# Column-tiled denominators, a layer norm scale moved into the residual, and a re-ordered head and tail in a linear-attention kernel

## The chip, the cores and the metric

The kernel runs on one core of a Trainium2 chip. The metric is device time in microseconds (us); lower is better. The engines are called TensorE (PE in the profile, its weight loads PEld), VectorE (DVE), ScalarE (ACT), GpSimd (POOL) and SyncE (SP, which issues 51 of the 53 DMA transfers that the profile of the kernel before lists).

One execution of a program on one core is called fast or slow by its time alone: slow is over 1.5% above the fastest run of the same kernel. Each run records its span on the core and the mean clock granted to TensorE, as a share of full speed. The product "span times (1 − granted clock)" is called the *clock loss* below: the time that TensorE would have had more at full clock. It is a derived number, not a measured delay, and E12 shows that part of it costs no time.

## The reference, cut to what matters

Two layers, each a linear attention (A) and a one-token feed-forward (B), on 2048 tokens of width 512, with 32 heads of 16.

```python
def _A_ref(x, wqkv, wo):
    q, k, v = ...                                    # x @ wqkv, split into 32 heads of 16
    phi = lambda t: jnp.where(t > 0, t + 1, jnp.exp(t)) + 1e-6
    pq, pk = phi(q), phi(k)
    kv = jnp.einsum("bhsd,bhse->bhde", pk, v)
    z = jnp.einsum("bhsd->bhd", pk)
    num = jnp.einsum("bhqd,bhde->bhqe", pq, kv)
    den = jnp.einsum("bhqd,bhd->bhq", pq, z)[..., None] + 1e-6
    return heads_back(num / den) @ wo
def _B_ref(x, w_r, w_gate, w_up, w_down):
    r = x @ w_r                                      # one token is chosen: the largest r
    ...                                              # gather it, y = (silu(xs@w_gate) * (xs@w_up)) @ w_down
    return x + scatter(y * sigmoid(r_sel))           # y is added to that token alone
x = A_x
x = x + _A_ref(_layernorm(x), A_wqkv, A_wo)
x = x + _B_ref(_layernorm(x), B_w_r, B_w_gate, B_w_up, B_w_down)
x = x + _A_ref(_layernorm(x), A_wqkv, A_wo)          # layer 1, as layer 0
x = x + _B_ref(_layernorm(x), B_w_r, B_w_gate, B_w_up, B_w_down)
```

## The kernel before: the parts that matter

Every operation is recorded with its engine; a printed list of numbers (`ORDER`) then fixes the order on each engine, and another the PSUM banks. So "moving" an operation means another list.

The denominators of 512 queries come from four matmuls that sum into one PSUM bank. The weights `Zr` are padded to 128 columns, so each matmul uses the full width (128*128 in the profile below) although it fills only 32 rows of the result that differ from zero.

```python
def den(e):
    for m in (3, 0, 1, 2):
        ins = e.matmul(B(db), Zr[:, m, :, :].rearrange("p a b -> p (a b)"), pqT[:, m, cols],
                       start=(m == 3), stop=(m == 2))
...                                     # then log and exp(-) on ScalarE: lden, rden
for m in range(NC_D):                   # per group: four broadcasts by matmul, four multiplies on VectorE
    A("pe",  ... e.matmul(B(bb), sel[:, m, :], rden[:, j, :], start=True, stop=True) ...)
    A("dve", ... e.tensor_tensor(pqT[:, m, cols], pqT[:, m, cols], B(bb), ALU.mult) ...)
```

A feed-forward returns its own input, the layer norm, with the one token changed, and that is added to the residual stream. So after layer 0's feed-forward (the middle layer norm) `x` is scaled and shifted on GpSimd, for all 16 tiles of 128 tokens; later layer 1's attention output is added on VectorE.

```python
# middle layer norm, GpSimd, 16 tiles: x = x * (1 + 1/sd) - mean/sd
A("pool", ... e.tensor_scalar(x_tok[:, t, :], x_tok[:, t, :], us[:, t:t + 1], nmr[:, t:t + 1],
                              op0=ALU.mult, op1=ALU.add) ...)
# residual of a layer, VectorE
A("dve", ... e.scalar_tensor_tensor(out=x_tok[:, t, :], in0=B(ob), scalar=1.0, in1=x_tok[:, t, :],
                                    op0=ALU.mult, op1=ALU.add, accum_out=s1[L][:, t:t + 1]) ...)
```

The last row of the output is turned from a column into one row of 512 by four matmuls, copied from PSUM, and stored at an index that SyncE first loads into a register.

```python
for c in range(NC_D):
    ins = e.matmul(B(ob)[0:1, c * P:(c + 1) * P], xout_col[:, c:c + 1], ident[:, :], start=True, stop=True)
e.tensor_copy(row_out[:], B(ob)[0:1, :])            # 1 x 512
e.reg_load(reg_sp, idxu[0:1, 0:1]); iv = e.snap(reg_sp)
e.dma_start(out_rows[bass.ds(iv, 1), :], row_out[0:1, :])
```

## Time and profile before

| | before |
|---|---|
| time, median of 3 runs | 185.92 us (185.80 to 185.97) |
| profiled run | 184.34 us, span 182.5 us, granted clock 0.947 |
| TensorE / VectorE / GpSimd busy | 165.0 / 138.3 / 88.2 us |

The page of the profile of the kernel before: the span; the busy time of each engine; TensorE's busy tenths and its granted clock in 40 slices of 4.56 us; and one costly group (line, engine, operation, output and inputs, shapes, count, then busy us and mean ns, then idle us before it and what ended it).

```profile
span 182.5 us, 3799 instructions
...
PE 165.0 (90%) x1379; PEld 87.0 (48%) x1398; DVE 138.3 (76%) x423; ACT 109.5 (60%) x275; POOL 88.2 (48%) x144
...
PE   7999999999999977999999999999999799971691
...
PEclk9999999999999999999999999699999999997555
...
L773 POOL TENSOR_SCALAR x_tok<-x_tok,us,nmr 128x512 bf16<-128x512 bf16 x16 | 12.2, 774 | 0.9 <-DVE stat L770 0.9
...
```

TensorE is busy 90% of the span, and the holes that show in its row are, with slices counted from 0, the first, 14 and 15 (64 to 73 us), 31 (141 to 146 us) and four of the last five. The clock row shows a 6 in one slice near 116 us and 5 at the end, which is half speed. The group at the end is the GpSimd scaling that the change takes away from 14 of the 16 tiles: 774 ns each.

Windows view of the kernel before: for each stretch its length, then busy us of each engine with the instruction count, then the granted clock, the DMA share and GB/s.

```profile
...
core 0: us, PE busy (x) PEld busy (x) DVE busy (x) ACT busy (x) POOL busy (x), PEclk, DMA share, GB/s
65.00:71.00 6.00, 3.85 (x17) 1.45 (x17) 5.49 (x18) 4.54 (x18) 0.00 (x0) 1.00 0.01 3
114.00:119.00 5.00, 4.76 (x109) 3.90 (x107) 1.89 (x5) 1.21 (x4) 1.99 (x4) 0.66 0.01 3
119.00:125.00 6.00, 5.92 (x78) 3.89 (x77) 4.35 (x16) 3.16 (x8) 1.30 (x3) 1.00 0.01 3
165.00:180.00 15.00, 7.97 (x239) 7.25 (x239) 9.18 (x49) 3.36 (x15) 6.75 (x13) 0.55 0.39 142
...
```

From 65 to 71 us TensorE is busy 3.85 of 6.00 us while VectorE is busy 5.49. Of the 2.15 us that TensorE is idle, 1.23 end when ScalarE delivers the reciprocal `rden` of a denominator group whose matmuls had just run, and 0.87 end with a broadcast multiply on VectorE. From 114 to 119 us the clock is 0.66: a part of this stretch ran at half. At 165 to 180 us, the tail, the clock is 0.55 and TensorE works on one-column matmuls.

Timeline of TensorE in the kernel before, at the first denominator group of layer 0 (start, duration, engine, line, operation, count). The four denominator matmuls overlap (each is recorded at 379 ns, the four together at 1.03 us), so what a group costs is the distance to the next start.

```profile
...
start us, us, engine line op out<-in xcount [idle before <-releaser]
...
54.78 1.03 PE L676 MATMUL ps<-pqT,Zr 128*128 128x512 bf16 x4
55.64 0.59 PE L564 MATMUL ps<-wo,kvT 128*128 128x512 bf16 x2
...
```

The next matmul starts 0.86 us after the group's start (55.64 − 54.78).

Timeline of the end of the kernel before:

```profile
...
178.02 0.16 DVE L1048 TENSOR_TENSOR xout_col<-xcol,ps 128x4 bf16<-128x4 f32 x1 [1.75 <-PE ps L871]
...
178.24 0.58 PE L1055 MATMUL ps<-ident,xout_col 128*1 128x128 bf16 x4 [0.25 <-DVE xout_col L1048]
178.86 0.68 DVE L1059 CAST row_out<-ps 1x512 bf16<-1x512 f32 x1 [0.68 <-PE ps L1055]
180.24 0.32 SPq L1065 DMA_DIRECT2D out_dram<-row_out  x1
```

After the column is ready at 178.18, the four matmuls, the copy of 1x512 (0.68 us) and the register load stand before the store at 180.24.

### The profile page before, as it was taken

The page shows a single profiled execution, that of the slowest core. Times are in us where ns is not written, and L with a number is a line of the kernel's source. Part 1 is how long each engine was busy: PE and PEld are TensorE (multiplying, and loading weights), DVE is VectorE, ACT ScalarE, POOL GpSimd, SP SyncE. Part 2 cuts the span into 40 slices and gives each one's busy share as a digit, 9 for nine tenths or more (in the row PEclk, how much of TensorE's full clock was granted, in tenths as well). Part 3 has the DMA queues.
Part 4 walks back from the last instruction along what each step waited for, and adds up shares of the span by engine and source line. Part 5 has one row for each costly group of instructions (what it writes and reads, how often), then busy time and mean ns, then how long its engine had stood idle before and what let it go on. Part 6 is the DMA issues. An engine that isn't in the chain of part 4 may idle for free.

```text
span 182.5 us, 3799 instructions
## 1 busy us (share of the span) xinstructions
PE 165.0 (90%) x1379; PEld 87.0 (48%) x1398; DVE 138.3 (76%) x423; ACT 109.5 (60%) x275; POOL 88.2 (48%) x144
## 2 busy tenths in 40 slices
PE   7999999999999977999999999999999799971691
PEld 2344455444454423444455458774454244440680
DVE  7866788865789989889587657367488989899811
ACT  2297556586659568888968653236668346496110
POOL 4359468955552103338999997316152120009320
PEclk9999999999999999999999999699999999997555
DMA  5999224799920000222442200000000000003630
GB/s 153 328 384 176 25 59 86 204 269 370 380 77 0 0 4 0 57 59 57 86 90 58 59 4 0 4 4 0 2 4 0 0 0 0 0 4 115 230 122 0
DMA packets 23107, 15.83 MB, mean 87 GB/s; under 512 B 15633, under 2 KB 21522, under 8 KB 22962
## 3 DMA queue, kind: packets, MB, share of 16 engines
q1 hardware_dynamic: 23010, 15.47, 29.8%
q0 software_dynamic: 80, 0.13, 0.7%
q8 instruction: 11, 0.18, 0.4%
q14 instruction: 6, 0.05, 0.1%
HBM read 9.83 MB, written 2.10 MB: 65 GB/s over the span
## 4 chain that ended last, share of the span: by engine, by line
PE 78%; DVE 8%; POOL 5%; ACT 3%; DMA 2%; issue 2%; DVEq 0%
PE ps L514 27%; PE ps L596 15%; PE ps L702 15%; PE ps L531 4%; PE ps L676 4%; PE ps L849 3%; POOL xn_tok L636 3%; PE ps L687 3%; DVE pqT L689 2%; PE ps L812 2%; DMA x_tok<-in_A_x_dram 2%; PE ps L871 2%; POOL Eb L494 1%; DVE st L643 1%; ACT junk L711 1%
## 5 line engine op out<-in xcount | busy, mean ns | idle before, releaser
L514 PE MATMUL ps<-wqkv,xnT 128*128 128x512 bf16 x247 | 58.8, 379 | 0.6
L494 POOL TENSOR_SCALAR Eb<-Eb 128x512 bf16<-128x512 bf16 x64 | 39.9, 630 | 40.2 <-ACT Eb L492 37.3
L492 ACT ACTIVATE Eb<-ps 128x512 bf16<-128x512 f32 x64 | 37.7, 597 | 22.6 <-PE ps L596 10.4
L514 PEld LDWEIGHTS ps<-wqkv,xnT 128*128 128x128 bf16 x256 | 23.6, 97 | 24.9 <-issue 0.2
L596 PE MATMUL ps<-xnT,wqkv 128*128 128x512 bf16 x122 | 31.3, 385 | 0.6 <-DVE pk L496 0.2
L702 PE MATMUL ps<-Mw,pqT 128*128 128x512 bf16 x125 | 29.1, 379 | 1.2 <-DVE pqT L689 1.1
L496 DVE SCALAR_TENSOR_TENSOR pk<-ps,Eb 128x512 bf16<-128x512 f32 x32 | 21.6, 687 | 10.4 <-POOL Eb L494 8.4
L496 DVE SCALAR_TENSOR_TENSOR pqT<-ps,Eb 128x512 bf16<-128x512 f32 x32 | 21.6, 686 | 7.1 <-POOL Eb L494 6.9
L521 ACT ACTIVATE va<-ps 128x512 bf16<-128x512 f32 x32 | 19.2, 600 | 9.0 <-PE ps L514 6.2
L711 ACT ACTIVATE junk<-x_tok 128x512 bf16<-128x512 bf16 x32 | 19.9, 622 | 7.0 <-DVE x_tok L707 6.5
L707 DVE SCALAR_TENSOR_TENSOR x_tok<-ps,x_tok 128x512 bf16<-128x512 f32 x32 | 21.7, 689 | 3.1 <-PE ps L702 1.9
L689 DVE TENSOR_TENSOR pqT<-pqT,ps 128x512 bf16<-128x512 bf16 x32 | 20.3, 680 | 1.2 <-PE ps L687 1.2
L702 PEld LDWEIGHTS ps<-Mw,pqT 128*128 128x128 bf16 x128 | 12.1, 97 | 15.7 <-DVE pqT L689 1.7
L596 PEld LDWEIGHTS ps<-xnT,wqkv 128*128 128x128 bf16 x128 | 11.9, 99 | 13.7 <-issue 1.0
L636 POOL TENSOR_SCALAR xn_tok<-x_tok,cs,nms 128x512 bf16<-128x512 bf16 x16 | 12.2, 773 | 12.3 <-DVE nms L756 11.7
L636 POOL TENSOR_SCALAR xn_tok<-x_tok,rs,nms 128x512 bf16<-128x512 bf16 x14 | 11.6, 840 | 8.0 <-DVE nms L655 4.8
L773 POOL TENSOR_SCALAR x_tok<-x_tok,us,nmr 128x512 bf16<-128x512 bf16 x16 | 12.2, 774 | 0.9 <-DVE stat L770 0.9
L531 PE MATMUL ps<-va,pk 128*128 128x129 bf16 x128 | 11.9, 227 | 0.3 <-DVE pk L496 0.3
L531 PEld LDWEIGHTS ps<-va,pk 128*128 128x128 bf16 x128 | 9.3, 101 | 4.9 <-DVE pk L496 0.5
L687 PE MATMUL ps<-rden,sel 128*128 128x512 bf16 x32 | 9.3, 381 | 2.0 <-ACT rden L683 1.2
L643 DVE BATCH_NORM_STATS2 st<-x_tok 128x6 f32<-128x512 bf16 x16 | 10.1, 674 | 0.1
L1034 POOL TENSOR_SCALAR xn_tok<-x_tok,us,stat 128x512 bf16<-128x512 bf16 x9 | 7.0, 790 | 3.1 <-DVE us L1026 2.9
(191 smaller groups left out, 193.4 us busy)
## 6 DMA issues: line engine op xcount, KB each, us to landing
out_dram<-xn_tok SPq DMA_DIRECT2D x8, 256.0 KB, 2.1
wu<-in_B_w_up_dram SPq DMA_DIRECT2D x2, 896.0 KB, 8.7
wd<-in_B_w_down_dram SPq DMA_DIRECT2D x2, 896.0 KB, 7.1
wg<-in_B_w_gate_dram SPq DMA_DIRECT2D x2, 896.0 KB, 11.5
wqkv<-in_A_wqkv_dram SPq DMA_DIRECT2D x3, 512.0 KB, 7.8
x_tok<-in_A_x_dram SPq DMA_DIRECT2D x1, 1024.0 KB, 9.9
x_tok<-in_A_x_dram SPq DMA_DIRECT2D x2, 256.0 KB, 3.5
x_tok<-in_A_x_dram SPq DMA_DIRECT2D x1, 512.0 KB
```

Of the source, the lines that this page charges most:

```text
L492: A("act", lambda e: e.activation(Eb[:, i, :], src(), ACTF.Exp), reads=[b, "table"], writes=[f"E{i}"], est=600, name=name + "E")
L494: A("pool", lambda e: e.tensor_scalar(Eb[:, i, :], Eb[:, i, :], 1.0, 0.0, op0=ALU.min, op1=ALU.max), reads=[f"E{i}"], writes=[f"E{i}"], es ...
L496: return A("dve", lambda e: e.scalar_tensor_tensor(out=dst, in0=src(), scalar=1e-6, in1=Eb[:, i, :], op0=ALU.max, op1=ALU.add), reads=[b, ...
L514: ins = e.matmul(B(b), xT[:, c, t * P:(t + 1) * P], wqkv[:, c, lo:lo + D], start=(c == 0), stop=(c == NC_D - 1))
L521: A("act", lambda e: e.activation(va[:, i, :].rearrange("p (m k) -> p m k", k=129)[:, :, 0:P], B(vb).rearrange("p (m k) -> p m k", k=P), A ...
L531: ins = e.matmul(views[m], pk[:, i, m * P:(m + 1) * P], va[:, i, m * 129:(m + 1) * 129], start=(first and m in (0, 3)), stop=False, skip_g ...
L596: ins = e.matmul(B(qb), wqkv[:, c, qc * P:(qc + 1) * P], xnT[L][:, c, tg * 512:(tg + 1) * 512], start=(c == 0), stop=(c == NC_D - 1))
L636: A("pool", lambda e: e.tensor_scalar(xn_tok[:, t, :], x_tok[:, t, :], scale[:, t:t + 1], nbias[:, t:t + 1], op0=ALU.mult, op1=ALU.add), r ...
L689: A("dve", (lambda e, m=m, bb=bb: e.tensor_tensor(pqT[:, m, cols], pqT[:, m, cols], B(bb), ALU.mult)), reads=[bb, f"pq{tg}_{m}"], writes=[ ...
L702: ins = e.matmul(B(ob), pqT[:, m, t * P:(t + 1) * P], Mw[:, m, :], start=(m == 0), stop=(m == NC_D - 1))
L707: A("dve", lambda e: e.scalar_tensor_tensor(out=x_tok[:, t, :], in0=B(ob), scalar=1.0, in1=x_tok[:, t, :], op0=ALU.mult, op1=ALU.add, accu ...
L711: A("act", lambda e: e.activation(junk[:, j, :], x_tok[:, t, :], ACTF.Square, accum_out=s2[L][:, t:t + 1]), reads=[f"x{t}", "table"], writ ...
```

## The change

The intent: give each of a group's four denominator matmuls 32 of the 128 columns, so that four run at once; take 14 of 16 scalings off GpSimd by folding the scale into the residual (and the shift into the last bias); start the first projection sooner; shorten the serial chains of the argmax, the feed-forward and the last row; and re-order everything. The diff, cut to its core (`...` marks cuts; the two number lists are replaced entirely):

```diff
-        Zr = SB("Zr", [P, NC_D, 4, 32], BF)
+        Zr = SB("Zr", [P, NC_D, 4, 8], BF)
...
-                for m in (3, 0, 1, 2):
-                    ins = e.matmul(B(db), Zr[:, m, :, :].rearrange("p a b -> p (a b)"), pqT[:, m, cols],
-                                   start=(m == 3), stop=(m == 2))
+                for m in range(NC_D):
+                    ins = e.matmul(B(db)[32 * m:32 * m + 32, :], Zr[:, m, :, :].rearrange("p a b -> p (a b)"),
+                                   pqT[:, m, cols], start=True, stop=True)
...   # head: token tiles 0 and 1 as separate loads, key weights on ScalarE's DMA queue
-        DMA("sp", x_tok[:, 0:2, :], ...); DMA("sp", wqkv[:, :, D:2 * D], ..., ["wk"], ...)
+        ldx("sp", 0, 1)
+        ldw("act", "wk", D)
...   # layer 1: the last two tiles take the residual from a matmul with the identity, statistics from PSUM
+                if xb:
+                    ins = e.matmul(B(ob), ident[:, :], x_tok[:, t, :], start=False, stop=True)
+            if xb:
+                bn = A("dve", lambda e: e.bn_stats(st6[:, t, :], B(ob)), ...)
+                A("act", lambda e: e.activation(x_tok[:, t, :], B(ob), ACTF.Identity), ..., after=[bn])
+            else:
+                scal = 1.0 if L == 0 else us1[:, t:t + 1]
+                A("dve", lambda e: e.scalar_tensor_tensor(out=x_tok[:, t, :], in0=x_tok[:, t, :], scalar=scal,
+                                                          in1=B(ob), op0=ALU.mult, op1=ALU.add, ...
...   # middle layer norm: scaling on GpSimd only for those two tiles
-            for t in ts:
-                A("pool", (lambda e, t=t: e.tensor_scalar(x_tok[:, t, :], x_tok[:, t, :], us[:, t:t + 1], ...
+            if big:
+                for t in ts:
+                    A("pool", (lambda e, t=t: e.tensor_scalar(x_tok[:, t, :], x_tok[:, t, :], usx[:, t:t + 1], ...
...   # argmax: one step fewer to the one-hot; totals as high and low bf16 halves
+            small(lambda e: e.scalar_tensor_tensor(out=oh_bf[:], in0=gi8[:, 0:1].to_broadcast([P, NT]),
+                                                   scalar=iota_p[:, 0:1], in1=oht[:], ...
-            A("pe", lambda e: e.matmul(B(tb)[:, 0:3], ones_mat[:, :], part[:, 0:3], start=True, stop=True), ...
+            A("pe", lambda e: e.matmul(B(tb)[:, 0:8], ones_bf[:, :], part_hl[:].rearrange("p a b -> p (a b)"), ...
...   # layer 1's feed-forward in two halves
+            parts = [(0, NFC)] if L == 0 else [(0, NFC // 2), (NFC // 2, NFC)]
...   # output tiles: GpSimd and ScalarE, no longer VectorE
-                    final_group(g, ["pool" if (t % 4) < 3 and t < 12 else "dve" for t in g])
+                    final_group(g, ["pool" if t < 11 else "act" for t in g])
...   # last row: one matmul, a copy of 4 x 128, the register loaded earlier
+            A("pe", lambda e: e.matmul(B(ob)[0:NC_D, 0:P], xout_col[:, :], ident[:, :], start=True, stop=True), ...
+            A("dve", lambda e: e.tensor_copy(row_out[:], B(ob)[0:NC_D, 0:P]), ...
+              ..., name="Rst", pre=row_reg, pre_after=[idx_op])
```

## The prediction

> **What bounds the kernel now.** The page gives TensorE 90% busy and the chain of waits gives it 78% of the span. Stretches cut from the windows view show three regimes.
> - Head, 0 to 9.9 us: first x load landed at 4.07, four statistics (2.47 us), then normalise on GpSimd (0.77 us a tile); the first projection starts at 9.74.
> - Middle, 9.9 to 161: matmuls nearly back to back (four 128x512 take 0.86 us). It leaks in two places: 65.5 to 71, where TensorE is busy 3.35 of 5.5 us, and 142 to 147 (3.82 of 5). In both VectorE is busy over 90%: the broadcast multiplies (680 ns) and residuals (689 ns) bind.
> - Tail, 161.1 to 182.5: a serial chain of small VectorE, ScalarE and one-column matmul work, with the granted clock at 0.50 from 168.
>
> **What the change does, and how much lies on the chain.**
> 1. Denominators: 8 groups of four full-width matmuls (0.86 us each group) become four 32-column matmuls into separate partition quarters.[...] I estimate 0.45 us a group: -0.4 us x 8. In layer 0 that is TensorE time (-1.6). In layer 1 VectorE binds, so there only the first group's latency counts.
> 2. Layer norm scale in the residual: removes 14 GpSimd operations of 774 ns (10.8 us) and adds about nothing to VectorE. GpSimd is 95% busy at 97 to 109, but TensorE is full there too: 0 to -0.5 us by itself.
> 3. Head: tiles 2 and 3 first, normalised on VectorE, key weights loaded by ScalarE's queue: -1.4 us.
> 4. Order: layer 0's denominators and broadcasts are spread among output matmuls, so the 65 to 71 leak shrinks (-1.2). In layer 1 the first denominator goes right after the kv transpose instead of three together: before, from rank-2 update (132.1) to first broadcast multiply (140.5) takes 8.4 us; I expect about 5.5 (-3).
> 5. Last two tiles: residual by an identity matmul (+0.43 us TensorE), statistics straight from PSUM; fewer moments ahead of the argmax. Before, 4.2 us pass between the last residual (163.7) and the max (167.9); I expect 2.5 (-1.7).
> 6. Argmax: 2.2 us to the gather becomes 1.6, as a 0.4 us output tile no longer sits inside it and one step goes (-0.6). Totals in bf16 halves instead of fp32 (0.57 us): -0.4.
> 7. FFN halves: removes the 0.3 us gap before the down matmuls: -0.3.
> 8. Final row: one matmul instead of four (-0.3), a 4x128 copy instead of 1x512 at 680 ns (-0.48), register load off the end (-0.5): -1.3.
>
> Sum: 1.6+1.4+1.2+3+1.7+1.0+0.3+1.3 = 11.5 us; I keep 11 because the intervals touch.
>
> **Prediction:** 185.9 - 11 = 174.9 us; 171.3 to 180 should hold it 8 times in 10. Faster by over 2%: 0.95; within 2%: 0.04; slower: 0.01.
>
> **What would show each step.** Denominator matmuls starting almost together, a group in under 0.6 us. First 128x512 projection near 8.3. GpSimd busy about 77 us. TensorE idle in the layer 0 output stage under 1 us. Rank-2 update to first broadcast multiply about 5.5 us. Last 512-wide matmul to end about 18 us rather than 21.4. Final copy about 0.2 us.
>
> **What would make it wrong.** Column tiles running one after another[...] (+2 to 3). The projection waiting for key weights on the second queue (+1). Low clock reaching further into the tail or the layer 0 FFN interleave. VectorE binding more of layer 1 than I read, so that the earlier start is given back (+2). ScalarE output tiles delaying the gate.

In step 1 the 0.45 us a group is the author's estimate, set against the 0.86 us measured in the profile of the kernel before; that the four tiles run at once was not yet shown by any run.

## The result, and the profile after

| | before | after |
|---|---|---|
| median | 185.94 us (4 runs, 185.80 to 186.02) | 178.08 us (4 runs, 176.53 to 180.61) |
| ratio of fast runs | | 0.9508, 95% interval 0.9489 to 0.9526 |
| profiled run | 184.34 us, span 182.5, clock 0.947 (fast) | 180.61 us, span 178.8, clock 0.932 (slow) |
| TensorE / VectorE / GpSimd busy | 165.0 / 138.3 / 88.2 us | 163.9 / 132.8 / 77.4 us |

A ratio is the mean time of one kernel's fast runs over the mean of the other's fast runs of the same rounds, so it is not quite the ratio of the medians in the table. The result is correct.

The changed kernel's five recorded runs are far apart, 176.53 to 180.61 us, with granted clocks from 0.968 down to 0.932, and the profiled one is the slowest. So this profile may be read for order and for durations of single operations, but not for how far down the time went.

The page of the changed kernel's profile, the same lines as before; the last line is now the VectorE residual that carries the scale.

```profile
span 178.8 us, 3791 instructions
...
PE 163.9 (92%) x1393; PEld 84.2 (47%) x1393; DVE 132.8 (74%) x415; ACT 112.3 (63%) x293; POOL 77.4 (43%) x127
...
PE   6599997999999999999999999999999989986393
...
PEclk9999999999999999999999999955799999999555
...
L744 DVE SCALAR_TENSOR_TENSOR x_tok<-x_tok,stat,ps 128x512 bf16<-128x512 bf16 x14 | 10.0, 735 | 0.0
...
```

GpSimd fell by 10.8 us, the size of the 14 scalings (77.4 was on record as about 77); its other work came out even, with two output tiles more. TensorE's hole near 65 us is gone, but its clock row has two 5s and a 7 in slices 26 to 28 (half clock from 117.1 to 127.3 us), where the kernel before has one 6.

Windows view of the changed kernel, the same stretches and one more at 30 us:

```profile
...
30.00:32.00 2.00, 0.93 (x5) 0.46 (x6) 1.84 (x4) 0.00 (x0) 2.00 (x4) 1.00 0.46 93
65.00:71.00 6.00, 6.00 (x31) 2.45 (x30) 6.00 (x20) 4.72 (x19) 0.99 (x2) 1.00 0.01 3
114.00:119.00 5.00, 5.00 (x125) 4.64 (x124) 2.86 (x10) 1.35 (x5) 1.29 (x3) 0.81 0.01 3
119.00:125.00 6.00, 6.00 (x78) 3.35 (x76) 1.53 (x7) 1.40 (x4) 0.61 (x1) 0.50 0.01 3
165.00:180.00 15.00, 7.08 (x235) 6.55 (x235) 6.28 (x40) 5.31 (x14) 2.50 (x4) 0.50 0.29 108
...
```

From 65 to 71 us TensorE is busy all 6.00 us. From 30 to 32 us it is busy only 0.93 us, in a place where the kernel before had no hole. And from 119 to 125 us the granted clock is 0.50.

Timeline of TensorE at the first denominator group of the changed kernel:

```profile
...
53.84 0.40 PE L700 MATMUL ps<-pqT,Zr 128*32 128x512 bf16 x4
54.17 0.60 PE L620 MATMUL ps<-xnT,wqkv 128*128 128x512 bf16 x2
```

The weights are now 128x32. One matmul is recorded with nearly the same duration (390 ns after, 379 ns before), but the next matmul starts 0.33 us after the group's start instead of 0.86.

Timeline of the end of the changed kernel:

```profile
...
175.46 0.16 DVE L1125 TENSOR_TENSOR xout_col<-xcol,ps 128x4 bf16<-128x4 f32 x1 [1.19 <-PE ps L932]
...
175.67 0.27 PE L1128 MATMUL ps<-ident,xout_col 128*4 128x128 bf16 x1 [0.25 <-DVE xout_col L1125]
175.98 0.28 DVE L1130 CAST row_out<-ps 4x128 bf16<-4x128 f32 x1 [0.36 <-PE ps L1128]
176.45 0.34 SPq L1140 DMA_DIRECT2D out_dram<-row_out  x1
```

One matmul, a copy of 0.28 us, and the store issues 0.83 us after the column's ready time (176.45 − 175.62) instead of 2.06.

### The profile page after: what moved, and what is told of

Its sections match the earlier page's. It is cut to its first block, busy times and chain, and to the rows that moved or that the text cites. A ratio compares the mean times of both kernels' runs of the same rounds, so it can differ in the third digit from the quotient of the medians.

```text
span 178.8 us, 3791 instructions
## 1 busy us (share of the span) xinstructions
PE 163.9 (92%) x1393; PEld 84.2 (47%) x1393; DVE 132.8 (74%) x415; ACT 112.3 (63%) x293; POOL 77.4 (43%) x127
## 4 chain that ended last, share of the span: by engine, by line
PE 63%; DVE 29%; DMA 3%; POOL 1%; issue 1%; ACT 1%; SPq 0%; POOLq 0%
PE ps L537 27%; PE ps L620 13%; PE ps L728 8%; DVE pqT L713 6%; DVE x_tok L744 5%; PE ps L554 4%; PE ps L906 3%; DMA x_tok<-in_A_x_dram 3%; DVE scr L480 2%; DVE pqT L506 2%; PE ps L932 2%; PE ps L711 1%; DVE st L667 1%; DVE Mw L594 1%; DVE pk L506 1%
## 5 line engine op out<-in xcount | busy, mean ns | idle before, releaser
L504 POOL TENSOR_SCALAR Eb<-Eb 128x512 bf16<-128x512 bf16 x64 | 39.4, 621 | 59.3 <-ACT Eb L502 50.0
L537 PE MATMUL ps<-wqkv,xnT 128*128 128x512 bf16 x256 | 60.3, 380 | 1.4 <-DVE pk L506 1.3
L620 PE MATMUL ps<-xnT,wqkv 128*128 128x512 bf16 x128 | 33.6, 402 | 0.1
L728 PE MATMUL ps<-Mw,pqT 128*128 128x512 bf16 x128 | 30.4, 379 | 0.8 <-DVE pqT L713 0.6
L750 ACT ACTIVATE junk<-x_tok 128x512 bf16<-128x512 bf16 x30 | 18.6, 621 | 7.8 <-DVE x_tok L744 7.7
L1112 POOL TENSOR_SCALAR xn_tok<-x_tok,us,stat 128x512 bf16<-128x512 bf16 x11 | 8.3, 772 | 13.6 <-DVE mv L777 9.0
L660 POOL TENSOR_SCALAR xn_tok<-x_tok,rs,nms 128x512 bf16<-128x512 bf16 x12 | 10.9, 915 | 0.4 <-DVE mv L669 0.2
L744 DVE SCALAR_TENSOR_TENSOR x_tok<-x_tok,ps 128x512 bf16<-128x512 bf16 x16 | 10.5, 680 | 0.0
L630 ACT ACTIVATE lnv<-mv,eps_col 128x2 f32<-128x2 f32 (+2 forms) x20 | 5.4, 289 | 8.1 <-DVE mv L669 5.6
L744 DVE SCALAR_TENSOR_TENSOR x_tok<-x_tok,stat,ps 128x512 bf16<-128x512 bf16 x14 | 10.0, 735 | 0.0
```

The source lines that it names most:

```text
L504: A("pool", lambda e: e.tensor_scalar(Eb[:, i, :], Eb[:, i, :], 1.0, 0.0, op0=ALU.min, op1=ALU.max), reads=[f"E{i}"], writes=[f"E{i}"], es ...
L537: ins = e.matmul(B(b), xT[:, c, t * P:(t + 1) * P], wqkv[:, c, lo:lo + D], start=(c == 0), stop=(c == NC_D - 1))
L620: ins = e.matmul(B(qb), wqkv[:, c, qc * P:(qc + 1) * P], xnT[L][:, c, tg * 512:(tg + 1) * 512], start=(c == 0), stop=(c == NC_D - 1))
L660: A("pool", lambda e: e.tensor_scalar(xn_tok[:, t, :], x_tok[:, t, :], scale[:, t:t + 1], nbias[:, t:t + 1], op0=ALU.mult, op1=ALU.add), r ...
L728: ins = e.matmul(B(ob), pqT[:, m, t * P:(t + 1) * P], Mw[:, m, :], start=(m == 0), stop=(m == NC_D - 1 and not xb))
L744: A("dve", lambda e: e.scalar_tensor_tensor(out=x_tok[:, t, :], in0=x_tok[:, t, :], scalar=scal, in1=B(ob), op0=ALU.mult, op1=ALU.add, acc ...
```

## The experiments

Twelve experiments were run: E1 to E4 on one chip, E5 to E8 on a second, E9 to E12 on a third, each set with 11 runs of the kernel before. "Profile" numbers below come from one profiled run each. All results were correct.

### E1: the changed kernel, unchanged (a control)

> The changed kernel again, for its fast state and its spread. Both theories: fast runs at 176.5 to 177.1 us, some runs at 179 to 181. If the slow runs are a matter of where the low clock falls, a fast trace has the stretch at granted clock 0.5 in the middle of the kernel (116.5 to 127 us in the slow trace) shortened to about 3.5 us, and everything else equal.

Six runs: 179.04 to 180.68 us, median 179.25, ratio 0.9757 (0.9691 to 0.9822). The same kernel that had been 5% faster was now hardly 2.5% faster, and called unclear. None of its runs reached the 176.5 of the first set. In its profile the granted clock is at half for 6.83 us from 118.3 to 125.1 us. In the first profile of the changed kernel it had been 10.24 us from 117.1, in the kernel before 3.41 us from 115.4. These are three, two and one times 3.41 us.

Such a stretch of 3.41 us at granted clock 0.50 is called a half-clock window below; the longer ones are counted as two or three. The records of the first two profiles give 3.413 us (before) and 10.240 us (after), and in them the clock is 1.00 or 0.50 and nothing between. What makes TensorE lose the clock was not shown; what these runs tell of it stands under E9.

### E9: the kernel before, unchanged

> The kernel before, unchanged, against itself, to test what its spread is made of. Theory A: its runs stand on steps, about 182.8, 184.2 and 185.9 us, and each step is one more stretch of 3.41 us at half clock in the layer 0 feed-forward stage, so the time less the clock loss (span times one minus the mean granted clock) is the same on every step, 174.6 within 0.6 us, and a profile that falls on the step at 182.8 shows no such stretch and its rank-2 update about 1.5 us earlier than the 132.07 of the first profile. Rival: the steps come from DMA or launch, then time less clock loss has the same spread as the time, and the profile shows the same single stretch on every step. Ratio against before 1.00 either way.

Six runs: 182.86 (clock 0.957), 184.22 (0.940), 184.26 (0.948), 184.46 (0.948), 184.53 (0.948), 185.97 (0.938); ratio 0.9977 (0.9921 to 1.0034). The profile fell on the lowest step, 182.86. Its windows in the same stretches:

```profile
...
114.00:119.00 5.00, 4.87 (x145) 4.43 (x144) 3.00 (x7) 1.21 (x4) 2.05 (x4) 1.00 0.03 7
119.00:125.00 6.00, 5.98 (x38) 3.24 (x38) 4.23 (x15) 3.96 (x10) 2.23 (x4) 1.00 0.00 0
...
```

The same instructions now ran at clock 1.00, where the first profile of the same kernel had 0.66 from 114 to 119. The rank-2 update that ends this stage starts at 130.53 instead of 132.07: 1.54 us earlier. TensorE is busy 4.87 of 5.00 us in that stretch by the profile, with 145 instructions, mostly one-column matmuls of the gather and the feed-forward. In the first profile of the kernel before, TensorE was busy 100% of the 3.41 us just ahead of its half-clock window, in E12 98%, with 95 and 82 one-column matmuls (the profile models where a matmul ends, so this busy share is itself an estimate). So a stretch that the profile calls busy can still lose the clock, and whether it does changes from run to run of one kernel.

The rival, that the steps come from somewhere else, falls: time less clock loss is 174.67 us on average over 39 runs of the kernel before, with a standard deviation of 0.56, while the time itself has 1.27. One run, 184.22 at 0.940, does not sit on its step; E12 shows what can do that.

### E12: the changed kernel once more

> The changed kernel once more as the control of this call. Theory A: times on steps near 176.7, 179.2 and 180.6 with granted clocks near 0.968 or 0.960, 0.950 and 0.932; time less clock loss 169.6 within 0.9, so about 5 us under the kernel before and not 9; the profile's landmarks up to layer 0's first max within 0.3 us of the first control's (108.43). Rival: the gain is 9 us and the slow runs are a disturbance, then time less clock loss also differs by about 9.

Six runs: 176.56 (0.968), 179.15 (0.950), 179.24 (0.941), 180.68 (0.932), 180.80 (0.934), 181.38 (0.931); median 179.96, ratio 0.9608 (0.9510 to 0.9706). Layer 0's first max is at 108.38, in E1 at 108.43. Over all 17 runs of the changed kernel (the five first ones, E1, E12) time less clock loss is 169.52 us on average, 5.15 below the kernel before, not 9. Its spread is 0.90 and not within 0.9 of 169.6 in every run (168.4 to 171.0): at high clock loss the corrected time is too low, because not all of that loss stands on the chain. The profiles of E1 and E12 show it: both have 6.83 us at half clock in the middle, but in the tail half clock begins at 166.1 us in E1 and at 163.3 in E12. Yet the spans are 177.46 and 177.44 us, and no stage of the tail differs by more than 0.02 us: 2.8 us more of half clock there cost nothing. So the correction is only approximate, and like is compared with like:

| | before | after | difference |
|---|---|---|---|
| mean of runs | 185.04 (39 runs) | 179.18 (17 runs) | −5.9 us, 3.2% |
| highest-clock step (before 0.957 to 0.958, after 0.959 to 0.968) | 183.09 (5 runs) | 176.72 (4 runs) | −6.4 us, 3.5% |
| the first comparison, fast runs (ratio 0.9508) | 185.94 (median) | 176.53 to 177.03 | about −9.1 us |

The first comparison set the kernel before on its step of 185.9 us (which goes with clock 0.937 to 0.940; the clock of those first unprofiled runs was not recorded) against the changed kernel on its highest-clock step. The change itself is worth about 6 us; some 3 us of the first ratio are a difference in the number of half-clock windows.

### E2: key weights back on SyncE's queue

```diff
-        ldw("act", "wk", D)
+        ldw("sp", "wk", D)
```

> The key weights go to SyncE's queue behind the x tiles 0 and 2 to 7, all else as changed. Theory A (the head gained nothing[...]): second statistics start near 5.0 instead of 6.46 us, first 128x512 projection near 8.2 instead of 9.66, and the time falls by 0.5 to 1.5 us. Theory B (the head is bound by all its bytes together, whichever queue): the first projection then waits for the weights and stays within 0.4 us of 9.66; the time stays within 0.4 us.

The control E1 first, then E2: VectorE's first statistics in the timeline.

```profile
...
4.39 0.69 DVE L667 BATCH_NORM_STATS2 st<-x_tok 128x6 f32<-128x512 bf16 x1 [0.79 <-DMA x_tok<-in_A_x_dram]
6.42 0.69 DVE L667 BATCH_NORM_STATS2 st<-x_tok 128x6 f32<-128x512 bf16 x1 [1.33 <-DMA x_tok<-in_A_x_dram]
```

```profile
...
3.98 1.29 DVE L667 BATCH_NORM_STATS2 st<-x_tok 128x6 f32<-128x512 bf16 x2 [0.38 <-DMA x_tok<-in_A_x_dram]
...
5.40 0.66 DVE L667 BATCH_NORM_STATS2 st<-x_tok 128x6 f32<-128x512 bf16 x1
```

In the control VectorE waits 0.79 and then 1.33 us for token tiles; in E2 the first two statistics run back to back, and the third starts at 5.40. The first 512-wide projection starts at 8.54 us instead of 9.62, the span is 176.2 instead of 177.5 with the same two half-clock windows in the middle, and the median is 178.01 against 179.25. So what the change gained in the head it lost again, about 1.1 us, by issuing the key weights on a second queue at 0.78 us. Loads of one tile took 6.1 us to land in the first profile of the changed kernel and 5.0 in E2. In that first profile, from 0 to 6.5 us, the packets of SyncE's queue take 46.1% of the time of the 16 DMA engines and those of ScalarE's queue 23.6%. E2 issues the weights later (behind the first three token loads, whose issue ends at 2.11 us in the first profile) as well as on another queue; no run separates the two.

### E3: denominators at full width in the changed kernel

```diff
-        Zr = SB("Zr", [P, NC_D, 4, 8], BF)
+        Zr = SB("Zr", [P, NC_D, NC_D, 4, 8], BF)     # zero outside the diagonal blocks
-                    ins = e.matmul(B(db)[32 * m:32 * m + 32, :], Zr[:, m, ...], pqT[:, m, cols], start=True, stop=True)
+                    ins = e.matmul(B(db), Zr[:, m, ...], pqT[:, m, cols], start=(m == 0), stop=(m == NC_D - 1))
```

> The changed kernel with the denominators as four full-width accumulating matmuls again (weights padded with zeros, so data, order and vector work are the same). Theory A (tiles run in parallel and TensorE time counts only where TensorE binds): a group goes back from 0.33 to 0.86 us, TensorE gets 4.2 us more work, and the time rises by 1.5 to 3 us, since in layer 1 VectorE binds. Theory B (all of it lies on the chain): rises by 4 us or more. Theory C (spread and earlier, they hide in gaps): under 0.7 us.

```profile
...
53.74 1.03 PE L703 MATMUL ps<-pqT,Zr 128*128 128x512 bf16 x4
54.61 0.81 PE L623 MATMUL ps<-xnT,wqkv 128*128 128x512 bf16 x3
```

The group takes 0.87 us again. Six runs: median 182.16 against 179.25 of the control, means 181.59 against 179.66 (+1.9), time less clock loss 172.20 against 169.31 (+2.9). Fast runs alone would give +0.7, but E3's three fast runs have a mean clock of 0.956 and the control's six 0.942, so that is not like with like. The cleanest comparison is of two profiles with the same 10.24 us at half clock in the middle: E3's span is 180.96 us, that of the first profile of the changed kernel 178.81 (+2.15). In the profile layer 0's max is 1.3 us later, rank-2 update to the first broadcast multiply 6.91 us instead of 6.41, and from there to the last output matmul of layer 1 22.29 instead of 21.75. So the column tiles pay about 2 us in the changed kernel (1.9 to 2.9 by these measures), and in layer 1 not only in the first group's latency.

### E4: column-tiled denominators alone, in the kernel before

```diff
-                    ins = e.matmul(B(db), Zr[:, m, ...], pqT[:, m, cols], start=(m == 3), stop=(m == 2))
+                    ins = e.matmul(B(db)[32 * m:32 * m + 32, :], Zr[:, m, ...], pqT[:, m, cols], start=True, stop=True)
```

> The kernel before with only the column-tiled denominators. A group takes 0.33 instead of 0.86 us. Theory A: layer 0 saves about 1 us where four groups stand in the TensorE stream and layer 1 about 1.5 us because three groups stand together before the first broadcast: 2 to 3 us faster (183 to 184). Theory B (VectorE absorbs it in both layers): under 0.7 us faster.

Six runs: median 182.44, mean 182.44 against 184.77 of the kernel before on that chip (−2.3), ratio 0.9884 (0.9808 to 0.9959). Time less clock loss falls by 2.4 (172.02 against 174.42). In the profile one half-clock window stands at 68.7 to 72.1 us, inside and behind the hole of 65 to 71 that the old order leaves (TensorE is busy 41% of the 3.41 us ahead of it), and one at 116.5 to 119.9. So this part alone gives over a third of the change's 6 us, and in this one profile clock 0.50 also fell in the hole. The hole is as deep in both profiles of the kernel before (TensorE busy 3.85 of 6.00 us from 65 to 71), at clock 1.00, so that the hole is the cause is not shown.

### E5: router-weight products moved off 24 to 29 us

The changed kernel computes four products of 128x512 for the second router on VectorE, back to back. From E12's timeline, VectorE and then TensorE:

```profile
...
24.67 1.11 DVE L480 SCALAR_TENSOR_TENSOR scr<-wo,wrc_bc 128x512 bf16<-128x512 bf16 x1
...
28.20 1.14 DVE L480 SCALAR_TENSOR_TENSOR scr<-wo,wrc_bc 128x512 bf16<-128x512 bf16 x1
...
```

```profile
...
31.06 1.04 PE L537 MATMUL ps<-wqkv,xnT 128*128 128x512 bf16 x4 [1.27 <-DVE pk L506]
...
```

TensorE stops for 1.27 us because the key features (`pk`) that it needs stand behind these products on VectorE. E5 moves the four products and their two followers to 85 to 105 us, where VectorE has idle time (it is busy 10.23 of 20.00 us there in the first profile of the changed kernel):

```diff
+        move("wow0", "A1k4phi"); move("wow1", "A1k5phi"); move("wow2", "A1k6phi"); move("wow3", "A1k8phi")
+        move("wowh", "A1k11phi"); move("wowl", "A1k10phi")      # each right behind the named operation
```

> The changed kernel with the four router-weight products (L480, 1.13 us each, back to back from 24.6 to 29.3 us) and the two small operations after them moved to the stage from 85 to 105 us, where VectorE has slack. Theory A (this block delays the key features and stops TensorE for 1.3 us near 30 us): the stop goes, the kv transpose of layer 0 comes 1.0 to 1.3 us before 53.5, and the whole is about 1 us faster, less what the middle stage waits for. Rival (TensorE has other work there or the middle stage swallows it): under 0.3 us at the argmax of layer 0 (108.4 in the control).

The kv transpose of layer 0 came 1.34 us earlier (52.14 against 53.48), but layer 0's max did not (108.75 against 108.43): from 79 to 93 us TensorE was now busy 13.08 instead of 13.83 of 14 us (E12), waiting for the same VectorE. Median 176.97, ratio 0.958 (0.9504 to 0.9655), but at a mean clock loss of 7.8 us against 10.3 in E1, so the lower time is the clock's: the profiles of E5 and E1, both with 6.83 us at half clock in the middle, have spans of 177.7 and 177.5. The stop was moved, not removed.

### E6: three query projections mixed into the feed-forward

```diff
+        move("A1q0_1", "B0g10"); move("A1q1_3", "B0u10"); move("A1q2_2", "B0u12")
```

> The changed kernel with three query projections (12 matmuls of 512 columns, 2.6 us) moved up from after the layer 0 FFN into it. Theory A (the granted clock falls to 0.5 for 3.4, 6.8 or 10.2 us[...]): low time in the middle is 3.4 us or none, slow runs become rare, and the median falls by 1.5 to 3 us. Rival (the fall of the clock has nothing to do with what is mixed in, or the later FFN result delays the chain behind it by as much): low time unchanged or time within 0.7 us of the control's 179.2.

The hope, a guess that no run had shown, was that 512-wide matmuls between the one-column ones would keep the clock. The profile has the same 6.83 us at half clock, only earlier (114 to 121). Median 178.60 at a mean clock loss of 7.8 us. With those windows equal its span is 0.55 us longer than E1's (178.01 against 177.46), and its rank-2 update is 0.55 us later, so the mixing has a price. It did not remove the windows in the profiled run; whether it makes them rarer cannot be told from six runs.

### E7: the last three GpSimd output tiles held until the last one-hot is written

```diff
+        move("Fx48", "B1oh"); move("Fx49", "Fx48"); move("Fx410", "Fx49")     # output tiles 8, 9, 10 on GpSimd
+        move("st8", "Fx49"); move("st10", "Fx410")                            # and their stores
```
with a dependency of the first of them on the one-hot.

> The changed kernel with the last three GpSimd output tiles held back until the one-hot column is written, so that GpSimd is idle while VectorE does the last argmax. Theory A (the small VectorE operations between max and gather stretch from 0.16 to 0.45 to 0.6 us[...]): L848 and L1094 fall to about 0.2 us, max to gather falls from 2.2 to 1.7 us, the end comes 0.4 to 0.6 us earlier. Rival (they wait for results[...]): 2.2 us stays within 0.1.

Small VectorE operations in the last argmax and GpSimd's output tiles, first in the changed kernel (its first profile), then in E7:

```profile
...
165.81 0.60 DVE L1094 TENSOR_SCALAR us<-stat 128x2 f32<-128x2 f32 x1
...
166.72 0.45 DVE L1094 TENSOR_SCALAR us<-stat 128x2 f32<-128x2 f32 x1
...
167.34 0.58 DVE L848 TENSOR_SCALAR oht<-iota,tif 128x16 f32<-128x16 f32 x1
...
```

```profile
...
165.62 2.28 POOL L1112 TENSOR_SCALAR xn_tok<-x_tok,us,stat 128x512 bf16<-128x512 bf16 x3 [0.40 <-DVE rt L1090]
```

```profile
...
161.74 0.15 DVE L1094 TENSOR_SCALAR us<-stat 128x2 f32<-128x2 f32 x1
...
162.19 0.14 DVE L1094 TENSOR_SCALAR us<-stat 128x2 f32<-128x2 f32 x1
...
162.58 0.22 DVE L848 TENSOR_SCALAR oht<-iota,tif 128x16 f32<-128x16 f32 x1
...
```

```profile
...
163.43 1.55 POOL L1112 TENSOR_SCALAR xn_tok<-x_tok,us,stat 128x512 bf16<-128x512 bf16 x2 [2.27 <-DVE psf L855]
```

With GpSimd at work until 167.9, a 128x2 or 128x16 `tensor_scalar` takes 0.45 to 0.60 us; with GpSimd idle it takes 0.14 to 0.22. Max to gather falls from 2.19 to 1.58 us, last output matmul to gather from 6.14 (E1) to 5.07. Part is given back, since small operations behind the gather now run beside the held tiles: a 128x4 copy (L872) takes 0.38 us instead of 0.17, a 128x1 operation for the index 0.57 (L1122) instead of 0.15, and gather to last down matmul is 7.24 instead of 6.92. The runs show the effect of GpSimd's work; why it stretches these operations they do not show. The run medians (176.16 here) are at a lower clock loss than E1's, 7.2 against 10.3, so the gain is read from the stage, about 0.8 us, and not from the medians. This profile had no half-clock window in the middle, and its rank-2 update starts at 130.18 us against 132.82 in E12, whose operations up to there are the same: two windows cost 2.6 us.

### E8: the scaling on GpSimd again

```diff
-                scal = 1.0 if L == 0 else us1[:, t:t + 1]
+                scal = 1.0
-            big = ts[0] in BT
+            big = True                  # scaling on GpSimd for all 16 tiles, placed behind the first argmax
```

> The changed kernel with the middle layer norm's scale and shift on GpSimd again for all 16 tiles (14 operations of 0.77 us, placed between the feature clamps after 108 us) and a constant 1.0 in the layer 1 residual. Theory A (GpSimd is not on the chain, and the register-scale residual costs VectorE 0.06 us a tile in the stage that VectorE binds): residuals fall from 735 to 680 ns, the layer 1 output stage is 0.5 to 0.8 us shorter, the clamps cost at most as much: the time within 1 us of the control, either way. Rival (the removed GpSimd work was on the chain): 1.5 us or more slower.

Groups by form in E8, VectorE's residuals:

```profile
...
L744 DVE SCALAR_TENSOR_TENSOR x_tok<-x_tok,ps 128x512 bf16<-128x512 bf16 x30 | 19.6, 677 | 0.0
...
```

All 30 residuals take 677 ns; in the changed kernel the 14 that read the scale from a 128x1 column take 735 ns. Over 14 tiles that is 0.8 us on VectorE, in the one stage where VectorE has no idle time (busy 21.70 of 21.70 us from 140.6 to 162.3 us in the first profile of the changed kernel); first broadcast multiply to last output matmul of layer 1 is 21.28 us in E8 and 21.75 in E1. On the other side, layer 0's max to gather is 2.93 instead of 2.33 us, since GpSimd works there again. The median is 181.73, but the profile has five half-clock windows (17.07 us), and time less clock loss is 169.73 against 169.52 of the changed kernel. So all that the runs show of the difference is clock, and I cannot give the folding of the scale a size of its own.

### E10: three mends together

```diff
-        ldw("act", "wk", D)
+        ldw("sp", "wk", D)
+        move("wow0", "Cxx"); move("wow1", "B0h_0"); move("wow2", "wow1"); move("wow3", "Cnvar")
+        move("wowh", "Cqphi"); move("wowl", "wowh")             # into VectorE's idle time at 112 to 130 us
+        ...                                                     # the five moves and the dependency of E7
```

> The changed kernel with key weights on SyncE's queue, the four router-weight products moved from 24.6 us into idle time of VectorE in layer 0's feed-forward stage (115 to 125 us), and the last three GpSimd output tiles held until the last one-hot is written. Theory A: these three act in different stages and add: first projection about 8.6, kv transpose of layer 0 about 51 (53.5 in the control), last output matmul to gather in layer 1 about 5.1 (6.1); span less clock loss 2.3 to 3.5 us under the control of the same call; median near 175.5. Rival: the earlier start is given back in layer 0's output stage, as it was when the products were moved to 85 to 105 us: the first max of layer 0 is earlier by under 1.2 us and span less clock loss falls by only 1.2 to 2.0.

Six runs: 175.02 to 177.79 us, median 175.67 against 179.96 of E12, means 176.06 against 179.63 (−3.6), ratio to the kernel before 0.9492 (0.9432 to 0.9553). Time less clock loss: 166.65 against 169.42 (−2.8). E10's and E12's profiles both have two half-clock windows in the middle, 6.83 us, and their spans are 173.9 and 177.4. First projection 8.74, kv transpose 51.26, layer 0's max 106.10 against 108.38, last output matmul to gather 5.07. So the gains add, and the rival falls: nothing was given back before layer 0's max, unlike in E5. The first of the products, at its new place:

```profile
...
112.11 0.69 DVE L480 SCALAR_TENSOR_TENSOR scr<-wo,wrc_bc 128x512 bf16<-128x512 bf16 x1
...
```

All four take 0.68 to 0.69 us there instead of 1.11 to 1.15, three of them with GpSimd idle throughout. This version beats both kernels.

### E11: two parts of the tail undone

```diff
-        BT = (14, 15)
+        BT = ()                        # residual on VectorE and squares on ScalarE for the last two tiles too
-            A("pe", lambda e: e.matmul(B(ob)[0:NC_D, 0:P], xout_col[:, :], ident[:, :], start=True, stop=True), ...
+            ...                        # four matmuls, a copy of 1x512, the register load just ahead of the store
```

> The changed kernel with two parts of its tail undone, all else in the same order: the last two tiles take their residual on VectorE and their squares on ScalarE again (no identity matmul, no statistics from PSUM), and the final row is copied as one row of 512 after four matmuls with the register load ahead as in the changed kernel. Theory A (the prediction's steps 5 and 8 are the causes): last output matmul of layer 1 to the max 5.0 to 6.0 us (3.95 in the control), last down matmul to the end 4.2 to 4.6 (3.42). Rival for step 5: it was the order of the moments, kept here, that shortened it: then at most 4.4. Median about 2 us over the control at the same clock.

One slip in that text: the register load was put back as in the kernel before, not left as in the changed one. Last output matmul to max: 4.68 us (E12 3.95, the kernel before 5.99). That lies between the theories' numbers: the identity matmul with statistics from PSUM gives 0.7 of the 2.0 us, and the rest is left to the order and the moments, which E11 kept and no run separates. Last down matmul to the end: 4.40 (E12 3.38, before 4.56), as expected. Four runs, 178.06 to 182.95, at clock losses from 7.9 to 14.9, median 181.81. Time less clock loss (169.34, E12 169.42) shows no cost at all, a miss of that measure: E11's profile has no half-clock window in the middle and 16 us in the tail, where 2.8 us more cost nothing in E12. Its span of 176.2 us stands 1.4 above the 174.8 that the stages below give the changed kernel without such windows.

## Why the prediction was right or wrong

The time, 178.08 us, lies in the range, and the direction was right. But the size was luck: with both kernels on their highest-clock step the gain is 6.4 us, which from 185.9 would have given 179.5, only just in the range. The prediction's sum was 11.5 us (11 kept). Stage by stage, from profiles without a half-clock window in the middle (E9 for before; E7 for after, up to layer 1's last output matmul, where it is the changed kernel; E12 from there on). "Last output matmul" and "last down matmul" mean their ends, and the identity matmul behind the last output matmul is not counted as one:

| stage | before | after | difference | predicted |
|---|---|---|---|---|
| start to first 512-wide projection | 9.51 | 9.71 | +0.2 | −1.4 |
| to the rank-2 update | 121.02 | 120.47 | −0.55 | −2.8 |
| to layer 1's first broadcast multiply | 8.44 | 6.40 | −2.0 | −3 |
| to layer 1's last output matmul | 21.40 | 21.74 | +0.3 | 0 |
| to the max | 5.99 | 3.95 | −2.0 | −1.7 |
| to the gather | 2.20 | 2.19 | 0.0 | −0.6 |
| to the last down matmul | 7.88 | 6.92 | −1.0 | −0.7 |
| to the end | 4.56 | 3.38 | −1.2 | −1.3 |
| sum | | | −6.2 | −11.5 |

The sum agrees with the 6.4 us between the highest-clock steps of the two kernels. The missing 5 us lie almost wholly before layer 1's first broadcast multiply.

1. **Denominators: right mechanism, size too small.** "0.45 us a group" was 0.33, a saving of 0.53 us in each of 8 groups. Done alone it gave 2.3 us (E4), undone alone about 2 (E3, 1.9 to 2.9), not 1.6 and a latency. That the four tiles run at once is shown by the 0.33 us, for one alone is recorded at 390 ns. No other cost of the tiles between full-width matmuls shows separately in the traces.
2. **Scale in the residual: "adds about nothing to VectorE" was wrong by 46 ns a tile.** The reading took the residual's duration with a constant, 689 ns in the kernel before. With a column as its scalar it takes 735 ns, in a stage where VectorE is busy without a break (21.70 of 21.70 us; E8, where the same form with a constant takes 677).
3. **Head: the failed step.** "First projection near 8.3" was 9.7. What was named as a risk, the projection waiting for key weights on the second queue, was the wrong wait: it was the statistics that waited for the token tiles, while the key weights were issued ahead of most of them (E2 moves the weights back: 8.54).
4. **Order: the 65 to 71 hole closed, and the gain went elsewhere.** TensorE is busy 6.00 of 6.00 us there, and idle 0.35 us from 54 to 85 us in E12 (2.26 in E9), under 1 us. But in the whole stretch from first projection to rank-2 update TensorE's busy time did not fall: 117.69 us in E9 and 117.65 in E11 (which is the changed kernel up to there). 2.5 us fewer of denominators (4.12 to 1.60) were filled by work that stood elsewhere before, such as the query column's projection (0.55 us, formerly behind the update) and transposes (0.16 to 0.94 us, formerly ahead of the first projection), and idle time fell only from 3.33 to 2.86 us, since a new stop of 1.27 us appeared at 30 us. E5 and E10 show that stop's cause, VectorE's four router products. The prediction saw the old holes and did not look in the new order for new ones. For the way to the first broadcast multiply, −2.0 of the predicted −3 came; 0.5 of it is the column tiles' (E3 and E4), the rest is left to the order.
5. **Last two tiles: the size is right, −2.0 for −1.7,** but only 0.7 us of it is the identity matmul with statistics from PSUM (E11).
6. **Argmax: not gained.** −0.6 was expected because VectorE's own output tile left it; GpSimd's output tiles, moved there, stretch the small operations by as much. Taking them away gives the expected 0.6 (E7: 1.58 us).
7. **Totals and halves: −1.0 for −0.7;** not separated by any run. The totals' matmuls are recorded at 0.57 us in fp32 before and 0.17 us in bf16 after.
8. **Final row: right, −1.2 for −1.3** (E11 puts 1.0 of it back).

What the prediction named as a danger, "low clock reaching further into the tail or the layer 0 FFN interleave", is what hid this error. Two or three windows of 3.41 us fall to half clock in that stage in the three profiles of the changed kernel, and none in E7 and E11, whose work up to there is the same. The first set of runs met the kernel before on its 185.9 step and the changed one partly on its 176.6 step, so the recorded difference was 7.9 us in the medians and 9.1 in the fast runs, for a change that is worth about 6.

## What to carry to other kernels

When a schedule is replaced, list the holes of the new order as well as the ones it closes: here a block of 4.7 us of VectorE work stopped TensorE, and weights issued early on a second DMA queue came with later landings of the loads that TensorE's first work needed. Before a difference of a few per cent is credited to a change, put both kernels' runs beside their granted clocks and compare runs on the same step, because here one stage with many one-column matmuls had none or one (before) and none to three (after) stretches of 3.41 us at clock 0.50, from one execution of the same work to the next; and look where the clock was lost, since two windows in layer 0's feed-forward cost 2.6 us here and 2.8 us more of half clock in the tail cost nothing. The serial argmax ran 0.6 us shorter with GpSimd idle (max to gather 1.58 us instead of 2.19), so work that can wait is best kept out of such a chain.
